# The sign of float64 weight words: a bit mask on VectorE, or a parametric ReLU on ScalarE

## The chip, the core and the metric

The kernel runs on one core of a Trainium2 chip. The metric is the device time of one execution in microseconds, from the first to the last instruction and a little around it. Three timed runs of the kernel before took 927.43, 928.60 and 929.07 us, median 928.6.

## The reference

The reference chains causal attention with a window and two feed-forward nets (FFN). Only what bears on the work is kept here:

```python
scores = where(mask, q @ k.T / sqrt(64) - slope[h] * abs(i - j), -1e9)   # 4 x 8 heads, 576 x 576, window 128
x = softmax(scores) @ v                                  # laid out as 2304 tokens x 512
h = x @ w_in                                             # first FFN: 512 -> 2048
x = (h * sigmoid(1.702 * h)) @ w_out                     # 2048 -> 512
g = x @ w_gate                                           # second FFN: 512 -> 1536
out = (g * sigmoid(g) * (x @ w_val)) @ w_out2            # 1536 -> 512
```

The products are wanted with more bits than one TensorE pass has. Each operand is split into a high and a low part, and three products are added (high by high, high by low, low by high). The weights arrive as float64 and have to become two float32 parts first.

## The kernel before

**Stages.** The 2304 tokens are 18 tiles of 128. Attention and the first FFN run over blocks of 4, 2, 4, 4 and 4 tiles, the second FFN over three groups of 6 tiles. Attention of block 0 comes first, that of block 1 runs beside the first FFN of block 0, and later attention beside the FFN of the block ahead. The second FFN is a stream of matmuls (L710) whose weights were prepared earlier and are read back from scratch memory.

**The weights of the first FFN** are 16 chunks, 0 to 15; a chunk is a piece of `w_in` and a piece of `w_out`, 512 KB each, loaded as words into the tile `wraw`. `split_steps` turns a chunk into two float32 parts in six steps, named w0 to w5 in the plan. ScalarE reads the high word of each float64 as a float32 and multiplies it by 2 to the power -112, which moves the exponent to where three shifts to the left make a float32 of it (w0, L194, Abs). VectorE masks the sign out of the high words, in place (w1, L196), puts the top bits of the low words beside it (w2, L198), and joins both with the shifted result of w0 (w3, L202). ScalarE rounds to the high part (w4, L207) and VectorE subtracts to get the low part (w5, L209).

**The weights of the second FFN** are prepared in units of a quarter of a chunk (`fraction`, L220 to L227, and what follows in `prepare`) while later attention and the first FFN run; `PACE` says how many steps are taken at a time.

**Order.** Each engine works its own queue in order. The opening, up to the eighth matmul group of the first FFN, is written out by hand in `PLAN`: S scores, F0 and F1 fold and minima, E0 and E1 exponentials, N reciprocals (L412, L413), P normalising on GpSimd (L419), T transposes (L451), C and L masks of the transposed tile, V attention products (L524), X and Z the two parts of their result, H and a to d one chunk's first product and its activation, Y its second product. So `T:1.0.0 F0:1.1.0 H:0.0` puts the transposes of block 1, head pair 0, group 0 in front of the first product of the first FFN (L559). The plan holds the splits of chunks 0 to 8. The splits of 9 to 15 are recorded after it, by `split_next`, and the framework's scheduler places them.

**Buffers.** A chunk's buffer is shared with an earlier tile. Those of chunks 8 to 11 hold the probabilities of block 0 until the attention products of a head pair have read them, those of 12 to 15 the same of block 1; only then is the chunk's load issued, by SyncE (L183). `yt`, through which results of the first FFN leave, has one buffer.

Of the kernel before, what the change touches and what calls it, by code (L numbers as in the profile page):

```python
# [8 lines left out]
F32 = mybir.dt.float32  # L9
# [3 lines left out]
AF = mybir.ActivationFunctionType  # L13
ALU = mybir.AluOpType
PSUM = bass.MemoryType.PSUM

P = 128
# [5 lines left out]
F0 = 8  # L23

CLOSE = 6

PACE = {0: 2.0, 2: 2.4, 3: 2.5, 4: 2.7}

REST = 74

LATE, PACE_LATE = 2, 0.8

O_SLOTS = 4

# [24 lines left out]
E1:0.0.1 N:0.0.1 E0:0.1.0 F1:0.1.0 P:0.0.1 N:0.0.0 E1:0.1.0 S:0.2.0 P:0.0.0 T:0.0.1 N:0.1.0 F0:0.2.0 C:0.0.1  # L59
P:0.1.0 T:0.0.0 w0:0 F1:0.2.0 L:0.0.1 T:0.1.0+2 E0:0.2.0 F0:0.1.1 S:0.3.0 E1:0.2.0 C:0.1.0 C:0.0.0 E0:0.1.1  # L60
L:0.0.0 N:0.2.0 F1:0.1.1 w0:1 P:0.2.0 V:0.0 F0:0.3.0 E1:0.1.1 F1:0.3.0 E0:0.3.0 T:0.2.0 S:0.2.1 X:0.0 N:0.1.1
w1:0 P:0.1.1 C:0.2.0 Z:0.0 E1:0.3.0 w2:0 F0:0.2.1 L:0.2.0 T:0.1.1+6 F1:0.2.1 E0:0.2.1 N:0.3.0 S:0.3.1 C:0.1.1
w3:0 P:0.3.0 E1:0.2.1 w1:1 w4:0 N:0.2.1 F0:0.3.1 L:0.1.1 T:0.3.0+6 F1:0.3.1 E0:0.3.1 P:0.2.1 V:0.1 w5:0 C:0.3.0
E1:0.3.1 w2:1 w0:2 N:0.3.1 w3:1 S:1.0.0 X:0.1 Z:0.1 w4:1 P:0.3.1 T:0.2.1 F0:1.0.0 C:0.2.1 L:0.3.0 T:0.3.1 w5:1
E0:1.0.0 w0:5 C:0.3.1 L:0.2.1 F1:1.0.0 V:0.3 w1:2 E1:1.0.0 V:0.2 w2:2 X:0.3 N:1.0.0 Z:0.3 P:1.0.0 w3:2 S:1.1.0
X:0.2 w1:5 w4:2 Z:0.2 T:1.0.0 F0:1.1.0 H:0.0 C:1.0.0 F1:1.1.0 E0:1.1.0 L:1.0.0 w5:2 E1:1.1.0 w2:5 w0:3 N:1.1.0
H:0.1 w3:5 P:1.1.0 a:0.0 b:0.0 w4:5 w1:3 c:0.0 w5:5 V:1.0 a:0.1 H:0.2 X:1.0 d:0.0 w0:4 b:0.1 w2:3 c:0.1 T:1.1.0
a:0.2 d:0.1 Y:0.0 C:1.1.0 w3:3 L:1.1.0 Z:1.0 w4:3 b:0.2 Y:0.1 w1:4 c:0.2 w5:3 w0:6 d:0.2 V:1.1 w2:4 S:1.2.0
w3:4 X:1.1 H:0.3 Z:1.1 w4:4 F0:1.2.0 F1:1.2.0 E0:1.2.0 Y:0.2 a:0.3 w5:4 E1:1.2.0 b:0.3 w0:7 S:1.3.0 N:1.2.0
w1:6 P:1.2.0 H:0.4 c:0.3 F0:1.3.0 F1:1.3.0 E0:1.3.0 T:1.2.0 a:0.4 H:0.5 d:0.3 C:1.2.0 b:0.4 E1:1.3.0 L:1.2.0  # L70
w2:6 c:0.4 Y:0.3 a:0.5 N:1.3.0 d:0.4 P:1.3.0 w3:6 V:1.2 b:0.5 w4:6 w1:7 Y:0.4 X:1.2 w5:6 c:0.5 Z:1.2 d:0.5
T:1.3.0 w2:7 Y:0.5 C:1.3.0 L:1.3.0 w3:7 H:0.6 w4:7 w5:7 V:1.3 a:0.6 H:0.7 X:1.3 Z:1.3 b:0.6 c:0.6 a:0.7 w0:8
b:0.7 d:0.6 c:0.7 d:0.7 w1:8 w2:8 w3:8 w4:8 w5:8
"""

SPREAD, LOAD_LAG, TRANSPOSE_LAG, VALUES_LAG = 0.65, 0.3, 4.0, 0.95
# [1 line left out]
QUARTERS = 1, 2  # L78

REBIAS = 2.0**-112  # L80


@with_exitstack
def attention_two_ffn(ctx: ExitStack, tc: tile.TileContext, q, k, v, w_in, w_out, w_gate, w_val, w_out2, yscr, wscr, woscr, out):
# [5 lines left out]
    nc = tc.nc  # L90
    H, _, _, D = v.shape
    NT = q.shape[1]
    S = 576
# [83 lines left out]
    w1 = {}  # L177
# [8 lines left out]
    def split_steps(raw):  # L186


        words, pool, tag = raw
        low, high = words[:, :, :, 0], words[:, :, :, 1]  # L190
        c = cvp.tile([P, 2, 512], U32, tag="cv", name="cv")
        cf = c.bitcast(F32)

        nc.scalar.activation(out=cf, in_=high.bitcast(F32), func=AF.Abs, scale=REBIAS)  # L194
        yield
        nc.vector.tensor_scalar(out=high, in0=high, scalar1=0x80000000, scalar2=None, op0=ALU.bitwise_and)  # L196
        yield
        nc.vector.scalar_tensor_tensor(  # L198
            out=low, in0=low, scalar=29, in1=high, op0=ALU.logical_shift_right, op1=ALU.bitwise_or
        )  # L200
        yield
        nc.vector.scalar_tensor_tensor(  # L202
            out=c, in0=c, scalar=3, in1=low, op0=ALU.logical_shift_left, op1=ALU.bitwise_or
        )
        yield
        t = pool.tile([P, 2, 2, 512], F32R, tag=tag, name="wt")
        nc.scalar.activation(out=t[:, :, 0, :], in_=cf, func=AF.Copy)  # L207
        yield
        nc.vector.tensor_tensor(out=t[:, :, 1, :], in0=cf, in1=t[:, :, 0, :].bitcast(F32), op=ALU.subtract)  # L209
        yield [t[:, 0], t[:, 1]]  # L210
# [4 lines left out]
    def fraction(raw, cs):  # L215

        low, high = raw[:, :, 0], raw[:, :, 1]
        cf = cs.rearrange("p s c -> p (s c)")[:, :512]
        c = cf.bitcast(U32)
        nc.scalar.activation(out=cf, in_=high.bitcast(F32), func=AF.Abs, scale=REBIAS)  # L220
        nc.vector.tensor_scalar(out=high, in0=high, scalar1=0x80000000, scalar2=None, op0=ALU.bitwise_and)
        yield
        nc.vector.scalar_tensor_tensor(
            out=low, in0=low, scalar=29, in1=high, op0=ALU.logical_shift_right, op1=ALU.bitwise_or
        )
        yield
        nc.vector.scalar_tensor_tensor(  # L227
            out=c, in0=c, scalar=3, in1=low, op0=ALU.logical_shift_left, op1=ALU.bitwise_or
        )
        yield  # L230
# [109 lines left out]
    def scores(j, hp, g):  # L340


        t0, n, lead = span(j)
        u = units[j, hp]
        tiles = tiles_of(j, g)
        m = len(tiles)
        sb = [bank("sb") for _ in range(2)]
        quarters = j >= QUARTERS[0]
        size = D if quarters else P
        for i in tiles:  # L350
            for c in range(0, P, size):

                lo = max(c, {"first": P, "after": D}.get(kind(t0 + i), 0))
                if c and kind(t0 + i) == "cross":
                    lo = P + D
                hi = P + c + size
                for e in range(2):
                    rows = slice(e * D, (e + 1) * D)
                    nc.tensor.matmul(  # L359
                        out=sb[e][c : c + size, (i % 2) * 256 + lo : (i % 2) * 256 + hi],  # L360
                        lhsT=u["q"][rows, i * P + c : i * P + c + size],
                        rhs=u["k"][rows, (i + lead - 1) * P + lo : (i + lead - 1) * P + hi],
                        start=True,
                        stop=True,
                        skip_group_check=quarters,
                    )
# [267 lines left out]
    w2, o2, p2 = {}, {}, {}  # L634
# [235 lines left out]
    def step(token):  # L870

        op, _, at = token.partition(":")
        at, _, fills = at.partition("+")
        at = tuple(map(int, at.split(".")))
        if op == "S":
            scores(*at)
        elif op in ("F0", "F1"):
            minima(*at, int(op[1]))
        elif op in ("E0", "E1"):
            exponentials(*at, int(op[1]))  # L880
        elif op == "N":
            reciprocals(*at)
        elif op == "P":
            normalise(*at)
        elif op == "T":
            transposes(*at, int(fills or 0))
        elif op in "CL":
            if op == "C" or at[0] or 2 * at[1] + at[2] not in ON_VECTOR:
                apart(*at, op == "L")
        elif op == "V":  # L890
            values(*at)
            valued[at[0]] += 1
            if at[0] == 1 and valued[1] <= H // 2 - 2:
                load_pair(1, valued[1] + 1)
            if at[0] == 0 and valued[0] == H // 2:
                load_w1(4)
        elif op in "XZ":
            take_x(*at, op == "Z")
        elif op in "Habcd":
            if op == "H":  # L900
                parts[at] = h_steps(*at)
            next(parts[at])
        elif op == "Y":
            y_part(*at)
        else:
            if op == "w0":
                splits[at] = split_steps(raw1[at[0]])
            done = next(splits[at])
            if op == "w5":
                w1[at[0]] = done  # L910

    E = mybir.EngineType
# [104 lines left out]
    for idx, (j, f) in enumerate(seq):  # L1017
# [118 lines left out]
```

## Time and profile before

| | us |
|---|---|
| median of three timed runs | 928.6 |
| the profiled execution | 926.68 |
| its span, first to last instruction | 924.9 |
| TensorE busy | 901.5 |
| VectorE busy | 717.1 |
| ScalarE busy | 453.6 |
| GpSimd busy | 123.2 |

PE is TensorE, DVE VectorE, ACT ScalarE, POOL GpSimd, SP SyncE (a q behind a name: its queue). Matmuls overlap, so a busy TensorE need not be one at its peak. A time in brackets behind a row is idle time in front of it, with what ended it. The granted clock of TensorE is given as a share of 2.4 GHz: 1.00 or 0.50 in a stretch of one level.

### The profile page before, as it was taken

What the parts mean: (1) busy time and instruction counts of PE and PEld (TensorE: products, weight loads), DVE (VectorE), ACT (ScalarE), POOL (GpSimd) and SP (SyncE); (2) the same over time, 40 slices, a digit from 0 to 9 for tenths busy, and PEclk for the clock granted to TensorE, in tenths of its full rate; (3) what the DMA queues carried; (4) which work ended last, traced back from release to release, by engine and by line L of the source; (5) the groups of instructions that cost most, each with busy time, mean ns of one, the idle gap of its engine ahead of it and who ended that gap; (6) DMA issues with size and microseconds to landing.
All of it is one profiled execution on the core that took longest, in us unless ns stands there. A gap on an engine that the chain in (4) does not pass through costs nothing.

```text
span 924.9 us, 15685 instructions
## 1 busy us (share of the span) xinstructions
PE 901.5 (97%) x5572; PEld 798.5 (86%) x5572; DVE 717.1 (78%) x1768; ACT 453.6 (49%) x1052; POOL 123.2 (13%) x221
## 2 busy tenths in 40 slices
PE   6899999999999999999999999999999999999998
PEld 4577898777777877788888899999899999999998
DVE  7898697877887678866748679899976679866777
ACT  5664566554554456544435445545444445344331
POOL 4744004412233013310000000000000000000000
PEclk8899999999999999999999999999999999999999
DMA  9954201545454465334573778988987677887764
GB/s 329 347 201 146 86 21 58 161 154 182 163 174 158 165 207 188 125 124 148 211 250 108 261 297 303 348 322 340 349 312 260 239 246 255 291 285 259 261 236 137
DMA packets 72462, 201.30 MB, mean 218 GB/s; under 512 B 6848, under 2 KB 38080, under 8 KB 65472
## 3 DMA queue, kind: packets, MB, share of 16 engines
q1 hardware_dynamic: 72384, 200.31, 61.1%
q8 instruction: 44, 0.72, 0.3%
q14 instruction: 34, 0.28, 0.1%
HBM read 156.76 MB, written 43.52 MB: 217 GB/s over the span
## 4 chain that ended last, share of the span: by engine, by line
PE 82%; DVE 8%; DMA 5%; ACT 2%; POOL 1%; issue 1%; SPq 0%; DVEq 0%; POOLq 0%; ACTq 0%
PE sx L710 15%; PE ox L710 8%; PE sz L710 8%; PE hp L559 6%; PE y L559 6%; PE y L561 6%; PE y L560 6%; PE hp L561 6%; PE hp L560 6%; PE sy L710 4%; PE oz L710 4%; PE oy L710 2%; PE xb L512 2%; PE sb L359 2%; PE pt L451 1%; DMA y_scratch<-yt 1%
## 5 line engine op out<-in xcount | busy, mean ns | idle before, releaser
L710 PE MATMUL sx<-ya,wg 128*128 128x384 f32 x864 | 171.9, 336 | 1.4 <-DMA wg<-w_scratch 1.4
L710 PEld LDWEIGHTS sx<-ya,wg 128*128 128x128 f32 x864 | 151.8, 188 | 1.8 <-DMA wg<-w_scratch 1.7
L559 PE MATMUL hp<-xh,wt 128*128 128x512 f32 (+1 forms) x320 | 121.1, 378 | 1.3 <-DVE yt L629 0.7
L561 PE MATMUL hp<-xh,wt 128*128 128x512 f32 (+1 forms) x320 | 118.1, 370 | 0.0
L560 PE MATMUL hp<-xl,wt 128*128 128x512 f32 (+1 forms) x320 | 118.0, 369 | 0.0
L560 PE MATMUL y<-gl,wt 128*128 128x512 f32 (+1 forms) x320 | 116.9, 371 | 0.5 <-DVE gl L590 0.5
L561 PE MATMUL y<-gh,wt 128*128 128x512 f32 (+1 forms) x320 | 117.1, 371 | 0.0
L559 PE MATMUL y<-gh,wt 128*128 128x512 f32 (+1 forms) x320 | 111.7, 377 | 1.0 <-DVE yt L623 0.5
L419 POOL TENSOR_SCALAR prob<-prob,stat 128x128 f32<-128x128 f32 x144 | 70.2, 506 | 209.8 <-DVE stat L413 66.4
L710 PE MATMUL ox<-p,wg 128*128 128x384 f32 x432 | 89.6, 337 | 1.1 <-DMA wg<-wo_scratch 1.1
L710 PE MATMUL sz<-ya,wg 128*128 128x384 f32 x432 | 88.3, 336 | 0.6 <-DMA wg<-w_scratch 0.6
L739 DVE TENSOR_TENSOR p<-th,p 128x384 fp32r<-128x384 f32 x126 | 68.1, 552 | 23.7 <-ACT p L738 23.0
L588 ACT ACTIVATE gh<-th 128x512 fp32r<-128x512 f32 (+1 forms) x80 | 46.7, 586 | 76.3 <-PE y L561 59.0
L590 DVE TENSOR_TENSOR gl<-th,gh 128x512 fp32r<-128x512 f32 (+1 forms) x80 | 51.5, 648 | 39.9 <-ACT gh L588 39.3
L738 ACT ACTIVATE p<-th 128x384 fp32r<-128x384 f32 x126 | 63.6, 520 | 35.7 <-DVE th L734 25.6
L710 PEld LDWEIGHTS ox<-p,wg 128*128 128x128 f32 x432 | 76.4, 188 | 1.5 <-DMA wg<-wo_scratch 1.4
L710 PEld LDWEIGHTS sz<-ya,wg 128*128 128x128 f32 x432 | 76.0, 188 | 1.0 <-issue 0.9
L559 PEld LDWEIGHTS hp<-xh,wt 128*128 128x128 f32 x320 | 60.3, 189 | 14.9 <-issue 1.6
L400 ACT ACTIVATE prob<-prob,stat 128x128 f32<-128x128 f32 x144 | 56.2, 392 | 33.0 <-DVE stat L384 32.7
L561 PEld LDWEIGHTS y<-gh,wt 128*128 128x128 f32 x320 | 60.3, 188 | 11.1 <-issue 1.0
L559 PEld LDWEIGHTS y<-gh,wt 128*128 128x128 f32 x320 | 57.3, 188 | 14.5 <-issue 2.6
L560 PEld LDWEIGHTS y<-gl,wt 128*128 128x128 f32 x320 | 60.4, 189 | 10.6 <-DVE gl L590 0.9
(96 smaller groups left out, 1583.0 us busy)
## 6 DMA issues: line engine op xcount, KB each, us to landing
wg<-w_scratch SPq DMA_DIRECT2D x36, 1024.0 KB, 5.3
wg<-w_scratch SPq DMA_DIRECT2D x36, 768.0 KB, 6.1
wg<-wo_scratch SPq DMA_DIRECT2D x18, 1024.0 KB, 6.4
wg<-wo_scratch SPq DMA_DIRECT2D x18, 768.0 KB, 7.8
w_scratch<-wa SPq DMA_DIRECT2D x24, 512.0 KB, 2.7
w_scratch<-wb SPq DMA_DIRECT2D x24, 384.0 KB, 3.1
wraw<-in_moe_w_in SPq DMA_DIRECT2D x16, 512.0 KB, 6.9
wraw<-in_moe_w_out SPq DMA_DIRECT2D x16, 512.0 KB, 7.8
```

Source lines behind the costliest of these rows:

```text
L359: nc.tensor.matmul(out=sb[e][c : c + size, (i % 2) * 256 + lo : (i % 2) * 256 + hi], lhsT=u["q"][rows, i * P + c : i * P + c + size], rhs= ...
L400: nc.scalar.activation(out=prob[:, x], in_=prob[:, x], func=AF.Exp, bias=stat[:, 0, x : x + 1], scale=-1.0, accum_out=stat[:, 1, x : x + 1],)
L419: (nc.vector if (j, hp, g) in NORM_ON_VECTOR else nc.gpsimd).tensor_scalar(out=prob[:, x], in0=prob[:, x], scalar1=stat[:, 3, x : x + 1], ...
L512: nc.tensor.matmul(out=x[r][e * D : (e + 1) * D, i * P + a : i * P + a + w], lhsT=u["v"][e][keys, kt + lead, :], rhs=u["pf"][keys].rearran ...
L559: nc.tensor.matmul(out=out_ap, lhsT=whi, rhs=xhi, start=start, stop=False)
L560: nc.tensor.matmul(out=out_ap, lhsT=whi, rhs=xlo, start=False, stop=False)
L561: nc.tensor.matmul(out=out_ap, lhsT=wlo, rhs=xhi, start=False, stop=stop)
L588: a = nc.scalar.activation(out=gh[:, :m], in_=th[:, :m], func=AF.Copy)
L590: d = nc.vector.tensor_tensor(out=gl[:, :m], in0=th[:, :m], in1=gh[:, :m].bitcast(F32), op=ALU.subtract)
L710: nc.tensor.matmul(out=bank_[:, :HT], lhsT=w[:, kk, at, a, :], rhs=p2[2 * (q // 2 - 1) + kk, i][:, b, :] if m == "O" else y2[q // NP2, i][ ...
L738: nc.scalar.activation(out=t[:, 0], in_=src, func=AF.Copy)
L739: nc.vector.tensor_tensor(out=t[:, 1], in0=src, in1=t[:, 0].bitcast(F32), op=ALU.subtract)
```

## The change

Abs becomes Prelu with the slope -(2^32) for negative numbers. A negative word then comes out positive and 2^32 times larger: its exponent field has a bit more, and the shift by three that follows in the join moves this bit to the place of the sign. The sign so travels with the exponent; the mask and the operation that put it beside the low words go. What is left of the two is a shift of the low words by 29, in place. It reads nothing that ScalarE reads or writes. A split has five steps, w0 to w4, instead of six; the tokens that were w2 leave the plan and the others keep their places. `fraction` has one step less, and the paces are scaled to it.

```diff
-PACE = {0: 2.0, 2: 2.4, 3: 2.5, 4: 2.7}
+PACE = {0: 1.8, 2: 2.1, 3: 2.2, 4: 2.4}
-LATE, PACE_LATE = 2, 0.8
+LATE, PACE_LATE = 2, 0.7
...
-w3:0 P:0.3.0 E1:0.2.1 w1:1 w4:0 N:0.2.1 F0:0.3.1 L:0.1.1 T:0.3.0+6 F1:0.3.1 E0:0.3.1 P:0.2.1 V:0.1 w5:0 C:0.3.0
+w2:0 P:0.3.0 E1:0.2.1 w1:1 w3:0 N:0.2.1 F0:0.3.1 L:0.1.1 T:0.3.0+6 F1:0.3.1 E0:0.3.1 P:0.2.1 V:0.1 w4:0 C:0.3.0
...
+NEGATIVE = -(2.0**32)
...
-        nc.scalar.activation(out=cf, in_=high.bitcast(F32), func=AF.Abs, scale=REBIAS)
-        yield
-        nc.vector.tensor_scalar(out=high, in0=high, scalar1=0x80000000, scalar2=None, op0=ALU.bitwise_and)
-        yield
-        nc.vector.scalar_tensor_tensor(
-            out=low, in0=low, scalar=29, in1=high, op0=ALU.logical_shift_right, op1=ALU.bitwise_or
-        )
+        nc.scalar.activation(out=cf, in_=high.bitcast(F32), func=AF.Prelu, scale=REBIAS, alpha=NEGATIVE)
+        yield
+        nc.vector.tensor_scalar(out=low, in0=low, scalar1=29, scalar2=None, op0=ALU.logical_shift_right)
         yield
         nc.vector.scalar_tensor_tensor(
             out=c, in0=c, scalar=3, in1=low, op0=ALU.logical_shift_left, op1=ALU.bitwise_or
         )
...
-            if op == "w5":
+            if op == "w4":
```

`fraction` is changed in the same way. The lines behind it move up by five: in the new kernel the Prelu is L197, the shift L199, the join L201, the low part L208, the reciprocal L408.

The order of VectorE's instructions before, at the end of the opening, from the two bit operations on chunk 2 (`wraw_138`) on; L412 and L413 make the reciprocals of block 1, head pair 0, and `xl_370` is a part of the attention's result. In brackets are the counters that a row waits for; DMAHW are those of transfers:

```order
L196 TENSOR_SCALAR wraw_138<-wraw_138 128x1024 [waits DMAHW5_49,DMAHW4_49]
L198 SCALAR_TENSOR_TENSOR wraw_138<-wraw_138 128x1024 [waits DVE_49]
L412 TENSOR_SCALAR stat_499<-stat_499 128x4 [waits Activation_49]
L413 RECIPROCAL stat_499<-stat_499 128x4 [waits DVE_49]
L548 TENSOR_TENSOR xl_370<-xb_529,xh_369 128x512 [waits Activation_49]
L202 SCALAR_TENSOR_TENSOR cv_470<-cv_470,wraw_138 128x1024
L196 TENSOR_SCALAR wraw_147<-wraw_147 128x1024 [waits DMAHW3_49,DMAHW2_49]
```

The same place of VectorE's queue now (`wraw_551` is chunk 9, `wraw_557` chunk 11, `wraw_147` chunk 5):

```order
L199 TENSOR_SCALAR wraw_138<-wraw_138 128x1024 [waits DMAHW5_49,DMAHW4_49]
L199 TENSOR_SCALAR wraw_551<-wraw_551 128x1024 [waits DMAHW7_49,DMAHW6_49,Pool_49]
L407 TENSOR_SCALAR stat_497<-stat_497 128x4 [waits Activation_49]
L408 RECIPROCAL stat_497<-stat_497 128x4 [waits DVE_49]
L543 TENSOR_TENSOR xl_370<-xb_527,xh_369 128x512 [waits Activation_49]
L201 SCALAR_TENSOR_TENSOR cv_468<-cv_468,wraw_138 128x1024
L199 TENSOR_SCALAR wraw_147<-wraw_147 128x1024 [waits DMAHW3_49,DMAHW2_49]
L543 TENSOR_TENSOR xl_370<-xb_539,xh_369 128x512 [waits Activation_49]
L199 TENSOR_SCALAR wraw_557<-wraw_557 128x1024 [waits DMAHW3_49,DMAHW2_49,Pool_49]
```

The long operation on chunk 2 is gone, and the shift of chunk 9 stands in its place, between chunk 2's shift and the reciprocals; before, the first bit operation on chunk 9 came some hundred rows later.

VectorE before, later in the plan, at the end of the minima of block 1, head pair 2 (`stat_798`; the ISA rows are its minima, `wt_795` is the low part of chunk 4):

```order
L329 COPY_PREDICATED sb_770<-later_72,sb_770 64x2x64 [waits DVE_49]
L384 ISA prob_797,stat_798<-sb_770,bias_71 128x128 [waits DVE_49]
L384 ISA stat_798 128x1
L384 ISA prob_797,stat_798<-sb_770,bias_71 128x128
L384 ISA stat_798 128x1
L209 TENSOR_TENSOR wt_795<-cv_694,wt_795 128x2x512 [waits Activation_49]
L582 SCALAR_TENSOR_TENSOR th_825<-th_825,hp_781 128x512 [waits Activation_49]
L412 TENSOR_SCALAR stat_798<-stat_798 128x4 [waits Activation_49]
L413 RECIPROCAL stat_798<-stat_798 128x4 [waits DVE_49]
```

And now (`wraw_1044` is chunk 13):

```order
L324 COPY_PREDICATED sb_764<-later_72,sb_764 64x2x64 [waits DVE_49]
L199 TENSOR_SCALAR wraw_1044<-wraw_1044 128x1024 [waits DMAHW7_49,DMAHW6_49,Pool_49]
L379 ISA prob_791,stat_792<-sb_764,bias_71 128x128 [waits DVE_49]
L379 ISA stat_792 128x1
L379 ISA prob_791,stat_792<-sb_764,bias_71 128x128
L379 ISA stat_792 128x1
L208 TENSOR_TENSOR wt_789<-cv_690,wt_789 128x2x512 [waits Activation_49]
L577 SCALAR_TENSOR_TENSOR th_819<-th_819,hp_775 128x512 [waits Activation_49]
L407 TENSOR_SCALAR stat_792<-stat_792 128x4 [waits Activation_49]
L408 RECIPROCAL stat_792<-stat_792 128x4 [waits DVE_49]
```

The shift of chunk 13 has come in front of the last minima. The shifts of chunks 10, 11, 12, 14 and 15 stand in the planned part in the same way, at other places. In TensorE's queue the planned part is unchanged.

## Rows read from the trace of the kernel before

**Rows 1.** The page: span; busy us and share of TensorE.

```profile
span 924.9 us, 15685 instructions
PE 901.5 (97%) x5572; PEld 798.5 (86%) x5572; DVE 717.1 (78%) x1768; ACT 453.6 (49%) x1052; POOL 123.2 (13%) x221
```

**Rows 2.** Stretches: us, busy us of each engine, granted clock, DMA share, GB/s.

```profile
18.20:25.00 6.80, 3.88 (x19) 2.41 (x20) 4.18 (x22) 5.38 (x21) 4.32 (x10) 0.50 1.03 414
38.70:45.50 6.80, 5.10 (x25) 2.92 (x26) 6.33 (x19) 3.52 (x10) 3.65 (x5) 0.50 0.99 321
49.00:97.00 48.00, 47.94 (x270) 37.29 (x271) 39.68 (x90) 26.10 (x56) 18.61 (x20) 1.00 0.47 163
97.00:143.00 46.00, 44.33 (x346) 41.36 (x345) 42.30 (x65) 27.32 (x46) 0.00 (x0) 1.00 0.09 35
420.00:925.00 505.00, 498.28 (x2722) 479.13 (x2720) 383.90 (x771) 220.65 (x451) 0.00 (x0) 1.00 0.73 261
```

**Rows 3.** Waits of TensorE, 0 to 60 us: total, times, longest.

```profile
PE xb L524 <- POOL pf L479: 6.1, 2, 4.4
```

**Rows 4.** Timeline of VectorE, 43 to 46 us: start, duration, instruction.

```profile
43.48 0.69 DVE L196 TENSOR_SCALAR wraw<-wraw 128x1024 uint32<-128x1024 uint32 x1
44.20 1.23 DVE L198 SCALAR_TENSOR_TENSOR wraw<-wraw 128x1024 uint32<-128x1024 uint32 x1
...
45.54 0.18 DVE L413 RECIPROCAL stat<-stat 128x4 f32<-128x4 f32 x1
```

**Rows 5.** Timelines of GpSimd (first row) and TensorE, 43 to 49 us.

```profile
45.91 2.96 POOL L419 TENSOR_SCALAR prob<-prob,stat 128x128 f32<-128x128 f32 x4 [3.43 <-DVE stat L413]
...
43.44 3.15 PE L524 MATMUL xb<-pf,qkv 128*64 128x256 f32 x22
...
48.24 1.03 PE L451 MATMUL pt<-ident,prob 128*128 128x128 f32 x3 [0.71 <-POOL prob L419]
49.02 0.48 PE L559 MATMUL hp<-xh,wt 128*128 128x512 f32 x1
```

**Rows 6.** Groups by line: count, busy us, mean ns, idle before, releasers.

```profile
L223 DVE SCALAR_TENSOR_TENSOR raw<-raw 128x512 uint32<-128x512 uint32 x36 | 25.4, 704 | 0.5
...
L198 DVE SCALAR_TENSOR_TENSOR wraw<-wraw 128x1024 uint32<-128x1024 uint32 x16 | 19.5, 1217 | 0.0
...
L194 ACT ACTIVATE cv<-wraw 128x1024 f32<-128x1024 f32 x16 | 18.4, 1159 | 7.7 <-DVE wt L209 4.8 <-DMA wraw<-in_moe_w_out 2.9
...
L221 DVE TENSOR_SCALAR raw<-raw 128x512 uint32<-128x512 uint32 x36 | 15.4, 428 | 14.0 <-ACT cs L220 13.7
...
L196 DVE TENSOR_SCALAR wraw<-wraw 128x1024 uint32<-128x1024 uint32 x16 | 11.2, 699 | 0.8 <-ACT cv L194 0.8
...
L400 ACT ACT_TABLE_LOAD x1 | 1.3, 1283 | 0.8 <-PEq L1119 0.8
```

**Rows 7.** Chunk 9's second transfer: its issue; us to landing of issues 39.2 to 40.

```profile
39.69 0.55 SPq L183 DMA_DIRECT2D wraw<-in_moe_w_out  x1
...
wraw<-in_moe_w_out SPq DMA_DIRECT2D x1, 512.0 KB, 8.2
```

**Rows 8.** Timeline of TensorE: products of block 1, pair 1; transposes of pair 2.

```profile
64.81 1.09 PE L524 MATMUL xb<-pf,vr 128*64 128x128 f32 x12
...
75.77 0.60 PE L451 MATMUL pt<-ident,prob 128*128 128x128 f32 x4
```

**Rows 9.** Chunk 13's second issue; us to landing, it and chunk 15's (near 94).

```profile
67.26 2.10 SPq L183 DMA_DIRECT2D wraw<-in_moe_w_out  x1
...
wraw<-in_moe_w_out SPq DMA_DIRECT2D x1, 512.0 KB, 7.1
...
wraw<-in_moe_w_out SPq DMA_DIRECT2D x1, 512.0 KB, 4.4
```

**Rows 10.** Timeline of VectorE: last minima and reciprocal of block 1, pair 2.

```profile
71.38 0.29 DVE L384 CUSTOM_DVE_ANT_0 prob<-sb,bias 128x128 f32<-128x128 f32 x1
...
73.74 0.18 DVE L413 RECIPROCAL stat<-stat 128x4 f32<-128x4 f32 x1
```

More of the change, by code (lines that the diff above doesn't have):

```diff
@@ L61 @@
 L:0.0.0 N:0.2.0 F1:0.1.1 w0:1 P:0.2.0 V:0.0 F0:0.3.0 E1:0.1.1 F1:0.3.0 E0:0.3.0 T:0.2.0 S:0.2.1 X:0.0 N:0.1.1
-w1:0 P:0.1.1 C:0.2.0 Z:0.0 E1:0.3.0 w2:0 F0:0.2.1 L:0.2.0 T:0.1.1+6 F1:0.2.1 E0:0.2.1 N:0.3.0 S:0.3.1 C:0.1.1
-w3:0 P:0.3.0 E1:0.2.1 w1:1 w4:0 N:0.2.1 F0:0.3.1 L:0.1.1 T:0.3.0+6 F1:0.3.1 E0:0.3.1 P:0.2.1 V:0.1 w5:0 C:0.3.0
-E1:0.3.1 w2:1 w0:2 N:0.3.1 w3:1 S:1.0.0 X:0.1 Z:0.1 w4:1 P:0.3.1 T:0.2.1 F0:1.0.0 C:0.2.1 L:0.3.0 T:0.3.1 w5:1
-E0:1.0.0 w0:5 C:0.3.1 L:0.2.1 F1:1.0.0 V:0.3 w1:2 E1:1.0.0 V:0.2 w2:2 X:0.3 N:1.0.0 Z:0.3 P:1.0.0 w3:2 S:1.1.0
@@ L66 @@
[L66 to L69, printed above, removed]
+w1:0 P:0.1.1 C:0.2.0 Z:0.0 E1:0.3.0 F0:0.2.1 L:0.2.0 T:0.1.1+6 F1:0.2.1 E0:0.2.1 N:0.3.0 S:0.3.1 C:0.1.1
@@ new lines @@
+w2:0 P:0.3.0 E1:0.2.1 w1:1 w3:0 N:0.2.1 F0:0.3.1 L:0.1.1 T:0.3.0+6 F1:0.3.1 E0:0.3.1 P:0.2.1 V:0.1 w4:0 C:0.3.0
+E1:0.3.1 w0:2 N:0.3.1 w2:1 S:1.0.0 X:0.1 Z:0.1 w3:1 P:0.3.1 T:0.2.1 F0:1.0.0 C:0.2.1 L:0.3.0 T:0.3.1 w4:1
+E0:1.0.0 w0:5 C:0.3.1 L:0.2.1 F1:1.0.0 V:0.3 w1:2 E1:1.0.0 V:0.2 X:0.3 N:1.0.0 Z:0.3 P:1.0.0 w2:2 S:1.1.0
+X:0.2 w1:5 w3:2 Z:0.2 T:1.0.0 F0:1.1.0 H:0.0 C:1.0.0 F1:1.1.0 E0:1.1.0 L:1.0.0 w4:2 E1:1.1.0 w0:3 N:1.1.0
+H:0.1 w2:5 P:1.1.0 a:0.0 b:0.0 w3:5 w1:3 c:0.0 w4:5 V:1.0 a:0.1 H:0.2 X:1.0 d:0.0 w0:4 b:0.1 c:0.1 T:1.1.0
@@ L70 @@
+a:0.2 d:0.1 Y:0.0 C:1.1.0 w2:3 L:1.1.0 Z:1.0 w3:3 b:0.2 Y:0.1 w1:4 c:0.2 w4:3 w0:6 d:0.2 V:1.1 S:1.2.0
+w2:4 X:1.1 H:0.3 Z:1.1 w3:4 F0:1.2.0 F1:1.2.0 E0:1.2.0 Y:0.2 a:0.3 w4:4 E1:1.2.0 b:0.3 w0:7 S:1.3.0 N:1.2.0
 w1:6 P:1.2.0 H:0.4 c:0.3 F0:1.3.0 F1:1.3.0 E0:1.3.0 T:1.2.0 a:0.4 H:0.5 d:0.3 C:1.2.0 b:0.4 E1:1.3.0 L:1.2.0
-w2:6 c:0.4 Y:0.3 a:0.5 N:1.3.0 d:0.4 P:1.3.0 w3:6 V:1.2 b:0.5 w4:6 w1:7 Y:0.4 X:1.2 w5:6 c:0.5 Z:1.2 d:0.5
-T:1.3.0 w2:7 Y:0.5 C:1.3.0 L:1.3.0 w3:7 H:0.6 w4:7 w5:7 V:1.3 a:0.6 H:0.7 X:1.3 Z:1.3 b:0.6 c:0.6 a:0.7 w0:8
@@ L73 @@
-b:0.7 d:0.6 c:0.7 d:0.7 w1:8 w2:8 w3:8 w4:8 w5:8
+c:0.4 Y:0.3 a:0.5 N:1.3.0 d:0.4 P:1.3.0 w2:6 V:1.2 b:0.5 w3:6 w1:7 Y:0.4 X:1.2 w4:6 c:0.5 Z:1.2 d:0.5
+T:1.3.0 Y:0.5 C:1.3.0 L:1.3.0 w2:7 H:0.6 w3:7 w4:7 V:1.3 a:0.6 H:0.7 X:1.3 Z:1.3 b:0.6 c:0.6 a:0.7 w0:8
+b:0.7 d:0.6 c:0.7 d:0.7 w1:8 w2:8 w3:8 w4:8
 """
@@ L219, in fraction @@
         c = cf.bitcast(U32)
-        nc.scalar.activation(out=cf, in_=high.bitcast(F32), func=AF.Abs, scale=REBIAS)
-        nc.vector.tensor_scalar(out=high, in0=high, scalar1=0x80000000, scalar2=None, op0=ALU.bitwise_and)
-        yield
-        nc.vector.scalar_tensor_tensor(
-            out=low, in0=low, scalar=29, in1=high, op0=ALU.logical_shift_right, op1=ALU.bitwise_or
-        )
+        nc.scalar.activation(out=cf, in_=high.bitcast(F32), func=AF.Prelu, scale=REBIAS, alpha=NEGATIVE)
+        nc.vector.tensor_scalar(out=low, in0=low, scalar1=29, scalar2=None, op0=ALU.logical_shift_right)
         yield
```

## The prediction

> **What bounds the kernel now.** I read four views, in this order. The page's busy shares come first: TensorE is busy for 97% of a span of 924.9 us [rows 1]. An average over stages does not say where a faster VectorE helps, so the busy times by stretch come next [rows 2]. From 420 us to the end TensorE is busy for 498 of 505 us, from 49 to 97 us for 47.94 of 48: there VectorE can be as fast as it likes and the end does not move. From 97 to 143 us TensorE is idle for 1.7 of 46 us while VectorE is busy for 42.3; VectorE holds it up a little. Before 49 us nothing of the first FFN runs yet, and the reader is to see two stretches there, 18.2 to 25 and 38.7 to 45.5 us, with the granted clock at 0.50, that is 1.2 GHz instead of 2.4.
>
> The waits of TensorE in the opening are for GpSimd, 6.1 us at the attention products, the longest 4.4 us [rows 3]; each fall of the clock starts during or shortly after an idle time of that kind. GpSimd in turn waits for the reciprocals of VectorE (L413). The timelines show the last link before the first FFN matmul. VectorE's bit operations on chunk 2 (43.48 and 44.20 us) stand in front of the reciprocal at 45.54 us [rows 4]. GpSimd scales the probabilities from 45.91 us on, TensorE transposes them at 48.24, and the first FFN matmul starts at 49.02 [rows 5]. From the reciprocal's end (45.72) to that matmul are 3.3 us, and all that TensorE does later queues behind it.
>
> **The change part by part.** Removed: per first-FFN chunk one scalar_tensor_tensor on VectorE, 16 of 1217 ns, and per second-FFN unit one of 704 ns, 36 times: 19.5 and 25.4 us of VectorE [rows 6]. Of the 36, none counts: they lie after 143 us, beside matmuls. Of the 16, three stand before 49 us, those of chunks 0, 1 and 2; the last is that of 44.20.
>
> Replaced: the bit mask (L196, 699 ns, and L221, 428 ns) by a logical shift with the same tile, stride and kind of instruction. No shift with one tensor stands in the trace; the mask is the nearest row, the scalar_tensor_tensor with its 1217 ns the other end. I take 699. Abs becomes Prelu, with one tensor and constants as before: I take L194's 1159 ns. Its row shows 2.9 us of waiting for a transfer and 4.8 for VectorE, so a tenth of a us more or less on each would be covered [rows 6]. The thinner paces keep the preparation's progress: 2.0/8 and 1.8/7 of a unit per call are 0.250 and 0.257. I take nothing for them.
>
> Moved, and this decides: the mask was in place on the words that Abs read, so it had to wait for Abs; the rows of both masks show waits for Abs, 0.8 us behind L194 and 13.7 behind L220 [rows 6]. The shift touches the low words alone and waits only for the chunk's transfer. Nothing but the data held the splits of chunks 9 to 15 behind the planned part, and in the new order their shifts stand far up in VectorE's queue, among the attention steps (both orders are in the section on the change). VectorE works its queue in order, so a shift whose chunk has not landed holds all behind it.
>
> First place: chunk 9's shift now stands right in front of the reciprocal. Its second transfer is issued at 39.69 us and lands 8.2 us later, at 47.9 [rows 7]; the DMA engines are busy for 0.99 of that stretch [rows 2], so a faster VectorE does not bring it earlier. VectorE gets there at 44.2 us or, with the operations removed ahead, earlier. After 47.9: the shift, 0.7, and the two small operations that end with the reciprocal, 0.3 (in the trace from 45.43, where the long operation ends, to 45.72 [rows 4]); the reciprocal ends at 48.9 instead of 45.7. What follows keeps its 3.3 us. **+3.2 us**, bounds 2.5 and 4. The removals in the opening earn nothing here: VectorE waits anyway.
>
> The clock: TensorE then has nothing but one group of scores and four transposes between its attention products (which end at 46.5 in the trace [rows 5], a little earlier with less on VectorE) and 52 us, a longer gap than either of those beside which the clock fell in the opening. A fall lasts 6.8 us in both rows [rows 2]. If it ends before 52.2 it costs nothing; if it lies wholly on the FFN matmuls it costs half, 3.4. I take the middle, **+1.7**. The Trainium skill says (TensorE: Matmul & The Clock Gate, What's actually happening) that an idle array falls back to half clock and that sustained work releases it; the trace agrees, with 0.50 in both stretches. By that rule alone the fall is sure, and the sum would take 3.4 here instead of 1.7.
>
> Second place: chunk 13's shift stands in front of the rest of the minima of the pair whose transposes start at 75.77 us. Its buffer is free when the products of 64.81 us end, at 65.90 [rows 8]. In the trace its second half is issued at 67.26 and lands 7.1 later, 8.5 after the products; chunk 15's second half, issued near 94 us, took 4.4 instead, which would make it 5.8 [rows 9]. After the landing: the shift 0.6, then what the trace has from 71.38 to the reciprocal's end at 73.92, 2.5, then from there to the transposes at 75.77, 1.9 [rows 8, 10]. That is 10.8 to 13.5 us behind the products, where TensorE needs 9.9 (65.90 to 75.77). **+2.2 us**, bounds 0.9 and 3.6. The other five early shifts I take at nothing. Chunks 10, 11 and 12 have landed, by the same addition, when VectorE, now 2 to 3 us late, comes to them; for chunks 14 and 15 VectorE may lose 1 to 2 us, and between 49 and 97 us it has 8.3 us of idle time to lose [rows 2].
>
> From 97 us on, a chunk needs two full operations on VectorE instead of four. TensorE's idle 1.7 us and some matmuls stretched by waits go. Bounds 0 and 3: **-2.0 us**.
>
> Sum: 3.2 + 1.7 + 2.2 - 2.0 = 5.1. The profiled execution took 926.68 us, the span and 1.8 around it; that makes 931.8. It lies 1.9 below the median of the timed runs, 928.6; on the median it is **933.7 us**.
>
> **The rivals.** *The transfer is there in time* (faster). If chunk 9's halves have landed when VectorE gets to the shift, the opening keeps what it saves: at least the 1.1 us of the operation at 44.20, at most the 3.6 of three; I take 2.2, and 2.0 after 97 us. That is 928.6 - 4.2 = 924.4. It decides for this case if the landing comes before about 44. For it: in a quiet stretch such a transfer takes 4.4 us [rows 9], which from 39.69 is 44.1. Against: the 0.99 busy share there and the 8.2 us. *It evens out*: the landing some 2 us sooner, no fall of the clock, and chunk 13 in time, give +1.2 - 2.0, about 928. *A change of activation tables* (much slower). The only table load costs 1283 ns [rows 6]. If Prelu lay in another table than Exp, Tanh and Copy, each of 52 Prelu would bring up to two loads, 104 x 1.28 = 133 us of ScalarE, some of it beside other work: over 960. Against it: the new order of ScalarE has one load, as the old. The Trainium skill says (ScalarE: Activation LUTs, What ACT_TABLE_LOAD costs) that every switch to another set costs a load and a drain, about 2.66 us; no run here shows a switch.
>
> **How the numbers follow.** The forecast has 0.82, the transfer in time 0.08, evening out 0.08, tables 0.02. The low ends of the forecast's terms sum to 2.5 + 0 + 0.9 - 3.0 = +0.4, the high ends to 4.0 + 3.4 + 3.6 - 0 = +11.0. All ends at once are unlikely; 928.9 to 938.5 leaves out the faster rival, the tables and the utmost. A change under 0.2%, 1.9 us, cannot be told from none: faster means under 926.7, slower over 930.5. Most of the evening out and the lowest of the forecast lie between. Faster 0.09, same 0.11, slower 0.80.
>
> **What would show it.** In the profile after: a wait of VectorE for a transfer of in_moe_w_out of 3 to 5 us, ended at about 48 us, in front of a shift (L199); the reciprocal right behind it; the first FFN matmul at about 52 us; a stretch at clock 0.50 around 50 to 58; a second wait of the shift near 75 to 80 us and a wait of TensorE's transposes for GpSimd behind it; from 97 to 143 us fewer waits of TensorE; from 420 us on no change. The shift at 0.7 us and Prelu at 1.16. The forecast is wrong if the first FFN matmul comes at 49 us or before, which is the faster rival, or if the transposes are not late the second time, which takes 2.2 off.

## The result and the profile after

The new kernel takes 933.69 us (median of 11 runs, 931.75 to 936.22); the kernel before, run beside it, 929.07 (11 runs). The ratio is 1.0055, interval 1.0038 to 1.0072: slower by 4.6 to 5.1 us. The profiled execution was the slowest of the 11, 936.22 us with a span of 934.3. A second profile of the same kernel, from the run e9 below, took 931.61 with a span of 929.7. Both are read here, since what they differ in is part of the answer.

The page, the groups of the changed lines and the stretches of [rows 2], in the first profile:

```profile
span 934.3 us, 15603 instructions
...
PE 904.1 (97%) x5572; PEld 801.1 (86%) x5572; DVE 676.8 (72%) x1716; ACT 452.2 (48%) x1052; POOL 117.3 (13%) x221
```

```profile
L197 ACT ACTIVATE cv<-wraw 128x1024 f32<-128x1024 f32 x16 | 18.3, 1152 | 6.1 <-DVE wt L208 3.5 <-DMA wraw<-in_moe_w_out 2.6
...
L199 DVE TENSOR_SCALAR wraw<-wraw 128x1024 uint32<-128x1024 uint32 x16 | 11.4, 715 | 13.4 <-DMA wraw<-in_moe_w_out 13.4
...
L395 ACT ACT_TABLE_LOAD x1 | 1.3, 1283 | 0.8 <-PEq L1114 0.8
```

```profile
54.79:59.60 4.81, 4.81 (x12) 3.78 (x13) 4.40 (x19) 2.50 (x10) 1.79 (x2) 0.50 0.03 9
49.00:97.00 48.00, 41.84 (x211) 31.68 (x212) 38.08 (x94) 24.07 (x51) 16.42 (x22) 0.86 0.36 127
97.00:143.00 46.00, 45.94 (x329) 42.50 (x329) 33.42 (x49) 28.85 (x46) 1.27 (x2) 1.00 0.20 75
```

VectorE is busy for 40.3 us less (717.1 in [rows 1]); the removed operations had 44.9 us by their own durations [rows 6], and most operations start about 0.1 us before the one ahead of them ends (the one behind the reciprocal of 50.76 us, below, starts at 50.85). Still the span is longer. The shift waits for transfers, 13.4 us in four places, where the mask had waited 0.8 us for ScalarE [rows 6]. From 49 to 97 us TensorE is busy for 41.8 of 48 us instead of 47.9, and the granted clock is at 0.50 for the first 4.8 us of the first FFN. There is still one table load, and a Prelu takes 1152 ns against 1159 of Abs.

VectorE at the first place, where [rows 4] has the bit operations on chunk 2 and the reciprocal; then GpSimd and TensorE, where [rows 5] has 45.91 and 49.02 us:

```profile
43.12 0.69 DVE L199 TENSOR_SCALAR wraw<-wraw 128x1024 uint32<-128x1024 uint32 x1
49.95 0.70 DVE L199 TENSOR_SCALAR wraw<-wraw 128x1024 uint32<-128x1024 uint32 x1 [6.13 <-DMA wraw<-in_moe_w_out]
...
50.76 0.18 DVE L408 RECIPROCAL stat<-stat 128x4 f32<-128x4 f32 x1
```

```profile
51.13 3.48 POOL L414 TENSOR_SCALAR prob<-prob,stat 128x128 f32<-128x128 f32 x4 [9.59 <-DVE stat L408]
```

```profile
51.56 0.47 PE L446 MATMUL pt<-ident,prob 128*128 128x128 f32 x1 [6.45 <-POOL prob L414]
...
54.79 0.78 PE L554 MATMUL hp<-xh,wt 128*128 128x512 f32 x1
```

The first FFN matmul starts 5.8 us later than before. Chunk 9's data come late, and GpSimd scales the probabilities in 3.48 us instead of 2.96. Chunk 9's second transfer, 8.2 us in [rows 7], takes longer: issued at 40.19 us, landing 9.6 us later.

```profile
40.19 0.61 SPq L186 DMA_DIRECT2D wraw<-in_moe_w_out  x1
```

```profile
wraw<-in_moe_w_out SPq DMA_DIRECT2D x1, 512.0 KB, 9.6
```

The second place, VectorE and then TensorE. The minima of [rows 10] stand behind the shift now:

```profile
81.03 0.69 DVE L199 TENSOR_SCALAR wraw<-wraw 128x1024 uint32<-128x1024 uint32 x1 [3.05 <-DMA wraw<-in_moe_w_out]
```

```profile
82.28 0.47 PE L554 MATMUL hp<-xh,wt 128*128 128x512 f32 x1 [1.45 <-DVE stat L379]
...
83.33 0.56 PE L556 MATMUL hp<-xh,wt 128*128 128x512 f32 x1 [0.34 <-DVE wt L208]
83.69 0.63 PE L554 MATMUL hp<-xh,wt 128*128 128x512 f32 x1
```

It is an FFN product that is late here, not the transposes of [rows 8]: its result takes over a bank (a piece of the memory that TensorE writes to) of scores that the minima have still to read, and the low part of its weights (L208) stands in VectorE's queue behind them. The 0.63 us of the matmul at 83.69 is the half clock again.

How far TensorE lags behind the kernel before, in us, by the starts of the same matmuls in two traces (paired matmuls, below); the place is the time in us in the trace before:

| place | first profile | second profile (e9) | forecast |
|---|---|---|---|
| first FFN matmul (49) | +5.8 | +5.1 | +3.2 |
| after the first FFN products (55) | +8.1 | +6.4 | +4.9 |
| after the second place (80) | +11.3 | +7.9 | +7.1 |
| at 205 | +9.7 | +5.7 | +5.1 |
| at 410 | +10.5 | +5.9 | +5.1 |
| at 700 | +9.4 | +4.8 | +5.1 |

### The profile page after: what moved, and what is told of

Read it like the earlier page. It is cut to its first block, busy times and chain, and to the rows that moved or that the text cites. A ratio compares the mean times of both kernels' runs of the same rounds, so it can differ in the third digit from the quotient of the medians.

```text
span 934.3 us, 15603 instructions
## 1 busy us (share of the span) xinstructions
PE 904.1 (97%) x5572; PEld 801.1 (86%) x5572; DVE 676.8 (72%) x1716; ACT 452.2 (48%) x1052; POOL 117.3 (13%) x221
## 4 chain that ended last, share of the span: by engine, by line
PE 87%; DMA 8%; DVE 2%; SPq 1%; ACT 1%; issue 0%; POOL 0%; DVEq 0%; ACTq 0%
PE sx L705 15%; PE ox L705 8%; PE sz L705 8%; PE hp L554 7%; PE y L554 7%; PE hp L556 7%; PE hp L555 7%; PE y L555 7%; PE y L556 6%; PE sy L705 4%; PE oz L705 4%; DMA wraw<-in_moe_w_out 4%; PE xb L507 2%; PE sb L354 2%; PE oy L705 2%; PE pt L446 1%
## 5 line engine op out<-in xcount | busy, mean ns | idle before, releaser
L554 PE MATMUL hp<-xh,wt 128*128 128x512 f32 (+1 forms) x320 | 122.2, 382 | 1.5 <-DVE stat L379 1.4
L556 PE MATMUL hp<-xh,wt 128*128 128x512 f32 (+1 forms) x320 | 119.7, 374 | 0.3 <-DVE wt L208 0.3
L414 POOL TENSOR_SCALAR prob<-prob,stat 128x128 f32<-128x128 f32 x144 | 67.6, 488 | 214.4 <-DVE stat L408 129.1
L585 DVE TENSOR_TENSOR gl<-th,gh 128x512 fp32r<-128x512 f32 (+1 forms) x80 | 51.9, 648 | 57.7 <-ACT gh L583 56.8
L554 PEld LDWEIGHTS hp<-xh,wt 128*128 128x128 f32 x320 | 61.3, 192 | 14.5 <-issue 3.1
L556 PEld LDWEIGHTS hp<-xh,wt 128*128 128x128 f32 x320 | 61.3, 192 | 11.7 <-DVE wt L208 0.8
L554 PEld LDWEIGHTS y<-gh,wt 128*128 128x128 f32 x320 | 58.1, 188 | 15.0 <-issue 1.8
L555 PEld LDWEIGHTS hp<-xl,wt 128*128 128x128 f32 x320 | 61.4, 192 | 9.9
```

The source lines that it names most:

```text
L414: (nc.vector if (j, hp, g) in NORM_ON_VECTOR else nc.gpsimd).tensor_scalar(out=prob[:, x], in0=prob[:, x], scalar1=stat[:, 3, x : x + 1], ...
L554: nc.tensor.matmul(out=out_ap, lhsT=whi, rhs=xhi, start=start, stop=False)
L555: nc.tensor.matmul(out=out_ap, lhsT=whi, rhs=xlo, start=False, stop=False)
L556: nc.tensor.matmul(out=out_ap, lhsT=wlo, rhs=xhi, start=False, stop=stop)
L585: d = nc.vector.tensor_tensor(out=gl[:, :m], in0=th[:, :m], in1=gh[:, :m].bitcast(F32), op=ALU.subtract)
```

## The experiments

Ratios are to the kernel before, run on the same chip. Two edits are shared by several kernels. `late` queues a chunk's shift on VectorE behind an instruction already recorded, without a wait:

```diff
-    def split_steps(raw):
+    def split_steps(raw, late=None):
...
-        nc.vector.tensor_scalar(out=low, in0=low, scalar1=29, scalar2=None, op0=ALU.logical_shift_right)
+        with tc.issue_after(late) if late is not None else ExitStack(): nc.vector.tensor_scalar(out=low, in0=low, scalar1=29, scalar2=None, op0=ALU.logical_shift_right)
```

**e1, all early shifts held back.**

```diff
-            w[i] = list(split_steps(raw[i]))[-1]
+            w[i] = list(split_steps(raw[i], marks["d"] if i >= 9 else None))[-1]
```

> The shifts of chunks 9 to 15 are queued on VectorE behind the last step of the activation recorded before them, so that none stands in the planned part; the rest is the new kernel. Theory A (VectorE held by early shifts): no wait of a shift for a transfer, the first FFN matmul at about 47 us (49.0 before, 54.8 in the profile of the new kernel), because the removed operations now show; with 2 us less from 97 to 143 us the time is 925 us, 923.5 to 927, below the kernel before. Rival B (Prelu, the new shift or the paces cost the time themselves): 931 to 934, with the waits gone all the same. Rival C (the transfers themselves became slower because VectorE frees buffers earlier): first FFN matmul at 49 or later, 928 to 931.

Measured 923.37 us, ratio 0.995 (0.9935 to 0.9964); the time is 0.1 us under the expected range. VectorE waits for no chunk between 30 and 145 us, and the first place (VectorE, then TensorE) reads:

```profile
43.45 0.18 DVE L408 RECIPROCAL stat<-stat 128x4 f32<-128x4 f32 x1
```

```profile
46.85 0.48 PE L554 MATMUL hp<-xh,wt 128*128 128x512 f32 x1
```

Theory A holds, rivals B and C fall: the same operations in a different place of one queue make the kernel faster than both others. What the shifts' places cost is the distance from 0.995 to 1.0055, 9.7 us.

**e2, chunk 9 alone held back** (`i == 9` in place of `i >= 9`).

> Chunk 9's shift alone is held back; those of 10 to 15 stay early. Theory A: the first FFN matmul at about 47 us and no half clock behind it; VectorE now comes to chunk 11's shift at about 48 us, before that chunk has landed (53 to 56 us), so a wait of 5 us or more stands there, most of it beside the first two FFN products; the wait of chunk 13's shift, 3 us, stays and delays the transposes of the third pair, 3.4 us with the clock's fall in the profile of the new kernel. 929 us, 926 to 932: 2 to 5 above the kernel with all shifts held. Rival: only the first place matters, then within 1 us of the kernel with all held. Rival B (the operations cost it): 931 to 934.

Measured 930.12, ratio 1.0028 (1.0013 to 1.0044), 6.8 us above e1. The first FFN matmul comes at 48.42 us, but chunk 11's shift now makes VectorE wait, and TensorE waits for the low part of a chunk's weights queued behind it:

```profile
52.80 0.69 DVE L199 TENSOR_SCALAR wraw<-wraw 128x1024 uint32<-128x1024 uint32 x1 [4.42 <-DMA wraw<-in_moe_w_out]
```

```profile
58.51 0.50 PE L556 MATMUL hp<-xh,wt 128*128 128x512 f32 x1 [2.65 <-DVE wt L208]
```

The time was inside the expected range, but the price above e1 was not: 6.8 us instead of 2 to 5. By paired matmuls with e1, 4.9 us of it arise at the first FFN products, where most of the wait for chunk 11 was expected to be covered, and 2.3 at the second place. Undoing one bad place alone wakes the next one.

**e3, chunk 9 alone early** (`i >= 10`).

> Only chunk 9's shift stays early, in front of the reciprocals; 10 to 15 are held back. Theory A: the wait for chunk 9's transfer (4 to 6 us), the first FFN matmul at 52 to 55 us and the half clock behind it stay; the waits near 70, 81 and 99 us go, with the late transposes near 82 us. 930.5 us, 929 to 932: 3.4 less than the new kernel. Rival (second place was covered): 933 to 934.

Measured 932.82, ratio 1.0054 (1.0035 to 1.0073): above the range, and as slow as the new kernel. The first place is there in full:

```profile
49.77 0.69 DVE L199 TENSOR_SCALAR wraw<-wraw 128x1024 uint32<-128x1024 uint32 x1 [6.23 <-DMA wraw<-in_moe_w_out]
```

```profile
54.09 0.77 PE L554 MATMUL hp<-xh,wt 128*128 128x512 f32 x1
```

Paired with e1's trace, TensorE lags by 9.0 us from 52 to 103 us, with nothing added at the second place, by 9.8 at 205 and by 10.1 at 700. The framework ordered the program behind the plan differently in e3, and 1.1 us is lost there. This run alone could not price the second place; e10 does.

**e4 and e5, identity products in front of the late transposes.** In the plan, with +44 (e4) and +20 (e5):

```diff
-X:0.2 w1:5 w3:2 Z:0.2 T:1.0.0 F0:1.1.0 H:0.0 ...
+X:0.2 w1:5 w3:2 Z:0.2 T:1.0.0+20 F0:1.1.0 H:0.0 ...
```

> The new kernel with 44 more 128x128 matmuls of the identity in front of the transposes of block 1, pair 0, whose bank nothing else uses then: they give TensorE work of about 4.8 us (109 ns each) in the 6.5 us in which it waits for VectorE. Theory A: the wait stays, the granted clock stays at 1.00 behind it, the 12 first FFN matmuls take 0.23 us each instead of 0.43: 2.3 us less than the new kernel, 931.4 (930 to 932.5). Rival (the clock falls anyway, in what is left of the gaps): no change, 933 to 934.5. Rival (the fills come in the way of the transposes where the transfer lands early): up to 1.5 slower.

> The new kernel with 20 identity products instead of 44: in the run with 44 one took 0.229 us, 10.09 us in all, and the transposes came at 55.7 us although the reciprocal was ready at 49.5; 20 take 4.6 us of the 6.5 in which TensorE waits. Theory A: the transposes follow the probabilities again, the clock stays up, the first FFN matmul comes 1 to 2 us sooner than with 44: ratio to before 1.0015 (1.000 to 1.0025), against 1.0029 with 44 and 1.0055 with none. Rival (what is left of the gap, about 2 us and the pauses between the transposes, lets the clock fall): 1.004 to 1.006.

e4 measured 930.61, ratio 1.0029 (1.0014 to 1.0045); e5 929.17, ratio 1.001 (0.9997 to 1.0024). In e4 the products took twice what was reckoned and delayed the transposes to 55.7 us (the stretch below is 44 of them, each two records); in e5 they do not. The first FFN matmul of e5 comes as late as in e9, but at full clock:

```profile
45.81 10.09 PE L287 MATMUL pt<-ident 128*128 128x128 f32 x88
```

```profile
54.19:58.00 3.81, 3.81 (x18) 3.14 (x19) 3.39 (x15) 1.56 (x6) 1.27 (x2) 1.00 0.07 25
```

```profile
54.16:58.00 3.84, 3.84 (x13) 3.06 (x13) 3.48 (x17) 2.00 (x8) 1.79 (x2) 0.66 0.04 12
```

The first fence is e4, the second e5, the third the same stretch of e9 (third but last column: the clock). So the wait costs twice: once by itself, and once because TensorE comes out of its idleness at half clock. The gain of e5, 0.0042 to 0.0045 or about 4 us, is more than the clock alone: in both kernels chunk 13's shift had moved behind the minima, so that the second place was gone as well (the clock 1.2 to 2.3 by the two profiles, the second place 1.7 by e10).

**e6, the transfer in time.** As e3, with the transfers for the second FFN issued behind chunk 11's, and chunk 9's shift tied to its place behind chunk 2's (`loaded` and `shifts` keep recorded instructions by chunk):

```diff
-            nc.sync.dma_start(out=to.rearrange("p a c w -> p a (c w)"), in_=src)
+            with tc.issue_after(loaded["w11"]): nc.sync.dma_start(out=to.rearrange("p a c w -> p a (c w)"), in_=src)
...
-            w[i] = list(split_steps(raw[i], marks["d"] if i >= 10 else None))[-1]
+            w[i] = list(split_steps(raw[i], marks["d"] if i >= 10 else shifts["w2"] if i == 9 else None))[-1]
```

> Only chunk 9's shift early, as in the run with 10 to 15 held back, and the four transfers of 256 KB for the second FFN (L250) issued behind chunk 11's instead of ahead of chunk 8's. VectorE's and TensorE's orders are the same. Theory A (the price of the first place is set by chunk 9's landing): its issue moves from 39.84 to about 37.2 us and 1 MB less stands ahead of it, it lands 2.6 to 4 us sooner than 49.8, and the first FFN matmul comes as much sooner; ratio to before 1.002 (1.000 to 1.003) against 1.0054. Rival (the landing is set by what comes beside it, the loads of chunks 10 and 11 and of q and k, which now go out sooner too): landing within 1 us of 49.8, ratio 1.0045 or more.

Measured 928.11, ratio 1.0001 (0.9988 to 1.0014): 4.9 us less than e3, with VectorE's and TensorE's orders the same. The two shifts (chunks 2 and 9) follow each other without a wait, and the matmul comes 5.9 us sooner:

```profile
43.41 1.29 DVE L199 TENSOR_SCALAR wraw<-wraw 128x1024 uint32<-128x1024 uint32 x2
```

```profile
48.22 0.48 PE L554 MATMUL hp<-xh,wt 128*128 128x512 f32 x1
```

This is the faster rival of the prediction made to happen at the first place: the early shift costs only its 0.6 us of VectorE once its data are there. By paired matmuls TensorE is 7.7 us ahead of e3 from 60 to 143 us, and 4.6 at the end. So e6 stays above e1: by 1.4 us at 143 and by 5.6 at the end. The later order that it shares with e3 does not explain all of that, since e3 loses only 1.1 us in that part. In e6's trace a wait of 1.0 us that both have (at 147.9 us) is followed by 3.4 us at clock 0.50, 150.3 to 153.7, which e3's does not have. Whether the loads that were put off have a part in the rest was not tested.

**e8, Abs in the place of Prelu,** all early shifts held back.

```diff
-func=AF.Prelu, scale=REBIAS, alpha=NEGATIVE)
+func=AF.Abs, scale=REBIAS)
```

> All early shifts held back and Prelu replaced by Abs in both places, so the signs of the weights are left out of the result. Theory A (Prelu takes what Abs took, and nothing waits for the difference): ratio to before 0.995 (0.9935 to 0.9965). Rival (Prelu is longer and ScalarE is waited for): 0.992 or less.

Measured 923.67, ratio 0.9956 (0.9941 to 0.9971), inside the expected range; an Abs takes the 1152 ns of the Prelu. The kernel leaves out the signs of the weights, so this is a reading of time alone: Prelu itself costs nothing that shows.

**e7 and e12, the second FFN's preparation as before,** all early shifts held back (`fraction`, `PACE` and `PACE_LATE` taken from the kernel before); **e11 is e1 again, beside e12; e9 is the new kernel again, and e10 holds back chunk 13 alone** (`i == 13`).

> All early shifts held back; the preparation of the second FFN (fraction, and the paces) as in the kernel before, with Abs, mask and the long operation, 25 us of VectorE more after 143 us. Theory A (none of the 36 counts): the same as with the new one, ratio to before 0.995 (0.9935 to 0.9965). Rival (they do lengthen waits of TensorE between 143 and 420 us): 0.997 or more.

> The new kernel once more, beside the next three on one chip. Its first profile was its slowest run of 11 (936.2, median 933.7) and showed a wait of 3.05 us of chunk 13's shift with 3.4 us lost by TensorE behind it. If the second place belongs to every run: the profile shows it again, with a run near the median. If it is a matter of when the transfer lands: a run near the median shows a shorter wait there, TensorE's loss 0 to 1.5 us, and the first place of 9 us (as in the run with chunk 9 alone early) makes nearly the whole difference to the kernel with all held. Ratio to before 1.0055 (1.004 to 1.007).

> The new kernel with chunk 13's shift alone held back. If the second place costs 2.2 us in every run, as the prediction had it: 0.0024 less than the new kernel in ratio, 1.003. If it only costs in some runs: 1.0045 to 1.006, within 0.001 of it.

> All early shifts held back, once more, beside the next one on one chip: ratio to before 0.995 (0.9935 to 0.9965), as the first time.

> All early shifts held back with the second FFN's preparation of before, once more. The first time it was 1.9 us above the kernel with the new preparation, in another call, while the two profiles differ by 0.5 us or less from 143 to 420 us. If the 36 operations count: 0.9965 to 0.998 again, 0.0015 or more above the run beside it. If they don't: within 0.001 of it.

e9: 934.40, ratio 1.0052 (1.0034 to 1.0069). e10: 932.43, ratio 1.0034 (1.0017 to 1.005). The difference, 1.7 us by the ratios and 2.0 by the medians, is the second place; the intervals overlap, so its size is a reading, but e9's trace has it, in a run below the median:

```profile
78.76 0.69 DVE L199 TENSOR_SCALAR wraw<-wraw 128x1024 uint32<-128x1024 uint32 x1 [2.57 <-DMA wraw<-in_moe_w_out]
```

```profile
80.02 0.47 PE L554 MATMUL hp<-xh,wt 128*128 128x512 f32 x1 [0.87 <-DVE stat L379]
```

The second place is in both profiles of this kernel; the half clock behind it (3.4 us long, from 83.65 us), and with it a loss of 3.4 instead of 1.5 us, is in the first alone. By e9 and e10 the price is 1.5 to 2.0, a little under the prediction's 2.2.

e7: 925.24, ratio 0.9971 (0.9956 to 0.9987), against 0.995 of e1. e12: 925.58, ratio 0.997 (0.9956 to 0.9985), against 923.94 and 0.9945 (0.9925 to 0.9964) of e11. Theory A falls: twice the old preparation cost 1.6 to 2.3 us. The intervals overlap within each pair, but both pairs point the same way, and e8, run beside e7, lies 1.6 under it. The first pair of profiles showed little of it (both were the fastest run of their kernel). TensorE's waits of the second pair, from 143 to 420 us, e12 and then e11:

```profile
PE y L558 <- DVE yt L622: 1.2, 1, 1.2
PE xb L511 <- DVE stat L383: 0.8, 1, 0.8
PE y L558 <- DVE stat L383: 0.7, 1, 0.7
```

```profile
PE y L554 <- DVE yt L618: 0.4, 1, 0.4
```

Behind 420 us e12 (first fence) has a wait for a reloaded weight, of 0.5 us, that e11 does not have. The kernel before has it too (0.6 us), and none of the eleven profiles with the new preparation:

```profile
PE sx L709 <- DMA wg<-w_scratch: 1.6, 1, 1.6
PE ox L709 <- DMA wg<-wo_scratch: 1.1, 1, 1.1
PE sz L709 <- DMA wg<-w_scratch: 0.5, 1, 0.5
```

```profile
PE sx L705 <- DMA wg<-w_scratch: 1.3, 1, 1.3
PE ox L705 <- DMA wg<-wo_scratch: 1.1, 1, 1.1
```

By paired matmuls the old preparation loses 1.0 us between 420 and 700 us in both pairs, as the kernel before does against both profiles of the new one. Between 143 and 420 it loses 0.4 us in the one pair and 2.6 in the other. Most of that difference is the clock: e12's trace has 3.4 us at 0.50 from 249.3 us on, behind its 0.8 us wait, which costs up to 1.7 us; e7's has the same three waits (0.7, 0.9 and 0.5 us) and no such stretch. The operations and the paces were not parted, so which of the two it is stays open.

## Why the prediction was right

The time forecast, 933.7, was met, and the mechanism is the one that it named: a shift that nothing but its transfer holds is queued early, and VectorE waits in front of the reciprocals. e1 shows that the place is the cause, e6 that the landing sets the price, e8 that Prelu is not in it. But two of its terms were off by about 2 us each, in opposite directions. That the sum came out to the tenth of a us is luck; the sign and the rough size follow from the mechanism.

*The first place, +3.2, was too small: 5.1 and 5.8 in the two profiles.* What failed is the landing at 47.9 us. The step "a faster VectorE does not bring it earlier" held; but the transfer's 8.2 us were carried over from one execution of another program, and it took 9.6 in both profiles of this one, which with its issue (39.60 us in e9, 40.19 in the first) ends at 49.2 and 49.8. Over all profiles the same transfer took 9.1 to 9.8 us in the six where VectorE waits for it (both of the new kernel, e3, e4, e5, e10) and 8.2 to 9.4 in the seven others with the same loads ahead of it. The DMA engines did not get slower: while the transfer was under way they were busy for 1.03 of the time at 352 GB/s before and 0.99 at 360 GB/s in the first profile, so about 3.5 MB went through instead of 2.9, and the transfer shared the engines with more bytes of other loads. Why more of them came in between stays open; the next chunk's issue, 3.0 to 4.7 us after it against 4.9 in the kernel before, does not order these times. Another 0.5 us is in what follows the reciprocal: 3.85 us to the matmul instead of 3.3, most of it in GpSimd's scaling.

*The clock, +1.7 with bounds 0 and 3.4:* 2.3 in the first profile (12 matmuls that start 0.43 us apart instead of 0.23), 1.2 in the second (6 of them). The fall was taken to last 6.8 us; it lasted 10.2 in the first profile (49.5 to 59.7 us) and 6.8 in the second (50.0 to 56.8). The middle of unknown ends was a fair choice; in e5, where TensorE had work in the wait, the half clock behind it is gone. One reading beneath it was loose: the second fall before, at 38.7 us, comes behind a wait of 1.8 us for VectorE's reciprocals, which ended at 36.0; the wait for GpSimd there, 39.6 to 41.3 us, begins after it. The Trainium skill (TensorE: Matmul & The Clock Gate, What's actually happening) has the idle array fall back and sustained work release it; e5 and e9 agree, at clocks 1.00 and 0.66 over the same stretch behind the same wait.

*The second place, +2.2:* 1.5 to 2.0 by e9 and e10. The wait was where the text put it, but what came late was an FFN product that needs a bank of scores and a low part of weights, both behind the shift on VectorE; the text looked for the transposes, which wait for nothing there. VectorE's queue held more that TensorE wanted than the one thing followed there. The other early shifts were not all in time: the first profile shows waits near 70 and 99 us too (chunks 12 and 14), 2.1 and 2.2 us, which TensorE's work covered: the lag does not grow there.

*From 97 us on, -2.0:* between 80 and 205 us the lag falls by 1.6 in the first profile and 2.2 in the second. The size is right; that the removed operations alone bring it is not shown, since in e1 and e11, which have the same operations less, TensorE gains only 0.8 us on the kernel before in that stretch.

*"Of the 36, none counts": wrong.* e7 with e1 and e12 with e11 put the new preparation at 1.6 to 2.3 us. The table of stretches in [rows 2] has a hole from 143 to 420 us, and the statement was made for just that stretch; behind 420 us TensorE's idle time was taken for none of VectorE's doing, and yet 0.5 us of a wait for reloaded weights went with the preparation that writes them. In the new kernel's own profiles 0.3 and 0.9 us of a gain appear between 205 and 700 us. This gain and, in the second profile, smaller losses to the clock and at the second place made up for what the first place cost more than forecast.

The rivals: the transfer was not in time, by about 6 us; there is one table load; evening out would have needed the landing that e6 arranged.

## What to carry to other kernels

Before counting what an operation costs, ask what used to hold it back: when an edit cuts the last dependence on another engine, the operation may be queued far ahead, and an in-order engine then waits for data that nobody wanted yet. Read the new queue order, and pin such an operation behind the work that must not wait (e1: a few words in three lines, 9.7 us, and faster than both kernels). When a queue stalls, follow everything behind the stalled instruction that the bound engine needs, and price the half clock after the idle time as well.

## What had not been expected of the hardware

The same 512 KB transfer took between 8.2 and 9.8 us in thirteen profiles with the same loads ahead of it, and 6.2 in e6 without 1 MB of them. A 128x128 float32 product of the identity took 0.229 us at full clock, where the transposes of the same shape start 0.11 us apart.
